# Attention, expert halves and MLP in one kernel: a weight load goes ahead in its queue, and five pieces of side work stand elsewhere in the order

## Chip, cores and metric

One core of one Trainium2 chip runs the whole program. The metric is device time in microseconds (us), the median of several runs; lower is better.

## What is computed

The reference, cut to what matters:

```
scores = matmul(q, k.T) / sqrt(64)                 # B 2, H 8, S 576, D 64
cum    = cumsum(log(clip(f, 1e-4, 1)), -1)
scores = where(causal, -1e9, scores + cum[:, None] - cum[None, :])
attn   = exp(scores - rowmax);  attn /= attn.sum + 1e-9
x      = (attn @ v) as (1152 tokens, 512)

p      = domain_probs / (domain_probs.sum + 1e-9)   # 1152 x 4
x      = sum over e of p[:, e] * (relu(x @ w1[e]) @ w2[e])      # 4 experts, F 1024

h      = x @ w_in                                   # 512 x 2048
out    = (h * sigmoid(1.702 * h)) @ w_out           # 2048 x 512
```

## The kernel before, in words

Products of fp32 numbers are made of three products in the fast rounded type fp32r: each operand is split into a rounded high part and the remainder (`xh`/`xl`, `whi`/`wlo`, `hh`/`hl`), and `high*high + high*low + low*high` is summed in PSUM. A split costs a rounding copy, mostly on ScalarE (ACT, `round_act`, L74), and a subtraction, mostly on VectorE (DVE, such as `wlo` at L263) or GpSimd (POOL). TensorE (PE) does all products; all other engines prepare its operands and take its results away.

The program has three stretches that overlap at their borders. **Attention** (to about 200 us) goes in passes of heads, in units of up to four query tiles. A unit runs through the stages scores (L674, PE), `max` (L704, DVE: adds the decay row `cb` or `cbs` and takes the row's maximum `mx`), `exp` (L720, ACT, with the row sum `sm`), `norm` (L727 and L728 on DVE, then the scaling of `e` on POOL, L730), transposes `t` (L748, PE) with their copies `ph` to SBUF (L74, ACT), the product with the values `x` (`emit_pv`, L793), and its split into `xh` and `xl` (L74 and L809). Stages of later units are issued among those of earlier ones. **Expert halves**: the four experts' hidden width of 1024 is cut in two, so that there are eight halves. They are gone through in visits (L153): 0 to 6 take a half with those token groups that the attention has finished, 7 to 9 (`v_exp` on) with two groups, 10 to 13 (`v_all` on) with all tokens. For each visit the weights `wa` (first product, L994 or L1032) and `wb` (second product, L1162) are loaded in four pieces `wst` of 512 KB in pairs (`load_pair`), and rounded to `whi` and `wlo` by `split_w` (L239). The visits 0 to 6 run among the attention's work. From visit 7 on ("joint") the first product is made by a scheme with fewer products from sums of weights (`sum_weights`, L276: four additions `sr` on POOL) and sums of tokens (`tr`, `th`, `tl`, L323 to L344), and its results are combined on DVE (`u` L1075 and L1078, `jc` L1038). Partial outputs are scaled by the token's share and added up in `acc` (L1204, L1206). **The MLP** follows; its weights are converted beforehand in small steps (`mlp_convert`, L420: `cvt`, `wf`, `cvd`) that are spread over the expert halves by a running account `cv_due`.

What sets the order: the program is written once, and each engine carries out its instructions in an order that a scheduler fixes when the program is built, from the written order and from explicit ties. `keep_order` ties one instruction behind another, `tc.issue_after` ties what is issued inside it behind an instruction, and `pin_turn` holds engines to the written order. On each engine, and in SP's queue of DMA issues, what comes later in that order can't pass what comes first, even if that still waits for a semaphore or for a free buffer.

Places that the steps below speak of: `prep_keys` (L582) splits the keys of a pair of heads (part 0 the rounding `ks`, parts 1 and 2 the subtractions for the two heads, on DVE and POOL, L593). `load_cum` (L613) loads the decay rows: two `cb` of 128 x 512 and one `cbs` in two halves, the latter into a single buffer that the pass before must have left. `attention` (L896) walks over the units and calls all of that at fixed distances (`first[k] == i + 2` is two units before a pair's first). `place` (L1348) puts side work at steps `g` of the joint products; the account of conversions is kept in the loop that emits the products (L1511).

```
for k in [k for k in nxt if first[k] == i + 2]:
    load_cum(*k)
```

Of the kernel before, what the change touches and what calls it, by code (L numbers as in the profile page):

```python
# [53 lines left out]
def attn_moe_mlp(ctx: ExitStack, tc: tile.TileContext, qk0, qk1, qk2, v0, vp, fg, dp, wa_moe, wb_moe, wa_mlp, wb_mlp, out):  # L54
# [6 lines left out]
    nc = tc.nc  # L61
# [177 lines left out]
    def split_w(kind, v_, g):  # L239
# [13 lines left out]
        if v_ == 1:  # L253
            acts = [j for j in nc.cur_bb.bb.instructions if j.engine == nc.scalar.engine]
            keep_order([first_act[0] if kind == "a" else acts[-2], acts[-1]])
        (wa if kind == "a" else wb)[v_, g] = (hi, lo)
# [338 lines left out]
    def prep_parts(p, h0):  # L595

        for part in range(3):
            prep_keys(p, h0, part)
# [14 lines left out]
    def load_cum(p, h0):  # L613

        cs, b, s0 = p
        st = pairs[p, h0]
        r = b * H + h0
        st["cb"] = [cb_p.tile([128, 512], F32, tag="cb", name="cb") for _ in range(2)]
        for g, cb in enumerate(st["cb"]):
            load(cb, cumd[r + g:r + g + 1, :512].to_broadcast([128, 512]))  # L620
        st["cbs"] = cbs_p.tile([128, S], F32, tag="cbs", name="cbs")
        for g in range(2):
            load(st["cbs"][64 * g:64 * g + 64], cumd[r + g:r + g + 1, :].to_broadcast([64, S]))
# [109 lines left out]
    def emit_tr(c, u):  # L733
# [7 lines left out]
        for k, (q0, off, w, _) in enumerate(todo):  # L741
# [3 lines left out]
            for k0, k1 in [(0, min(nk, 4))] + [(4, 5)] * (nk > 4):  # L745
# [4 lines left out]
                for j, h in enumerate(hs if w == S else hs[k:k + 1] if len(hs) > 1 else hs):  # L750
                    r = 64 if w == S else 128
                    ph = ph_of[c, h]
                    ph = ph[:, 3:4, 0:64] if k0 else ph[:, 0:k1, o:o + r]
                    if plain(c) and k1 == 2 and h < 4:
                        nc.vector.tensor_copy(ph, cols[:, :, j * r:(j + 1) * r])
                    else:
                        round_act(ph, cols[:, :, j * r:(j + 1) * r])

# [137 lines left out]
    def attention():  # L896
# [16 lines left out]
        for i in range(len(seq) + L_X2 + 1):  # L913
# [5 lines left out]
            with tc.issue_after(last_pool) if i == 0 else ExitStack():  # L919
                for k in new:  # L920
                    prep_parts(*k)
# [13 lines left out]
            for k in [k for k in nxt if first[k] == i + 2]:  # L935
                load_cum(*k)
            for k in [k for k in nxt if first[k] == i and i]:
                load_values(*k)
            for k in names:
                j = i - STAGES[k]  # L940
                if k in per_unit:
                    if 0 <= j < len(seq):
                        per_unit[k](*seq[j])
                    continue
# [403 lines left out]
    def place():  # L1348
# [6 lines left out]
        for v_ in range(v_exp, v_all):  # L1355
            b, (c1, c2) = visits[v_]
            h0, h1, l2 = (3, v_, b, c1), (3, v_, b, c2), (4, v_, b, c1)
            put(h0, 1, sum_weights, v_ + 1, 0)
# [59 lines left out]
    for i, (kind, v_, b, c) in enumerate(seq):  # L1418
# [24 lines left out]
        for g in range(n_steps):  # L1443
# [58 lines left out]
            if late:  # L1502

                if sums_at.get(u, 0) < 2:
# [6 lines left out]
                    if kind == 3 and v_ in both_joint and c == EXP[0]:  # L1511
                        cv_due[0] += g in (0, 2)
# [69 lines left out]
```

## Time and profile before

| what | value |
|---|---|
| median of 3 runs | 687.19 us (686.39 to 687.92) |
| the profiled execution | 687.35 us |
| its span, first to last instruction | 685.6 us |
| PE busy | 675.8 us (99%) |
| DVE busy | 526.8 us (77%) |
| ACT busy | 350.7 us (51%) |
| POOL busy | 239.4 us (35%) |
| mean granted TensorE clock | 1.00 |
| moved | 87.6 MB, mean 128 GB/s |

The times lie 1.75 us above the span because a run holds some work around the first and the last instruction. Busy shares are means over stretches of different kinds. A row of a timeline gives the start, the duration, the engine, the line of the program, the operation with its output and inputs, how many were taken together, and in brackets how long the engine had been idle before it and what ended the idling. Names of tiles leave out their numbers.

### The profile page before, as it was taken

How to read it: one execution, taken by the hardware profiler on the slowest of the kernel's cores; microseconds unless marked ns; L12 is line 12 of the kernel's file. 1: busy time of each engine (PE TensorE's matmuls, PEld its weight loads, DVE VectorE, ACT ScalarE, POOL GpSimd, SP SyncE). 2: the span in 40 equal slices, each digit the busy share in tenths (PEclk: the TensorE clock that was granted, in tenths of full speed). 3: DMA queues.
4: the chain of work that ended last, by engine and by line, in shares of the span. 5: the costliest groups of instructions: out<-in, count | busy, mean ns of one | idle time of the engine just before them, and what ended most of it. 6: DMA issues, size and time to landing. Idle time of an engine off the chain costs nothing.

```text
span 685.6 us, 10990 instructions
## 1 busy us (share of the span) xinstructions
PE 675.8 (99%) x3886; PEld 594.8 (87%) x3886; DVE 526.8 (77%) x1088; ACT 350.7 (51%) x816; POOL 239.4 (35%) x302
## 2 busy tenths in 40 slices
PE   8999999999999999999999999999999999999997
PEld 5698789888888898898898898898999998998986
DVE  6787877788697768776988879767699889997532
ACT  5677777776642645644336253362547453562420
POOL 6766588562333464533135323132003400120000
PEclk9999999999999999999999999999999999999999
DMA  8965754334341135153531423413332445441012
GB/s 255 325 251 199 255 187 160 106 101 139 123 119 66 58 97 169 44 180 100 169 108 49 152 77 110 125 50 98 110 109 77 168 124 162 132 155 60 1 46 93
DMA packets 41127, 87.59 MB, mean 128 GB/s; under 512 B 3784, under 2 KB 5840, under 8 KB 40816
## 3 DMA queue, kind: packets, MB, share of 16 engines
q1 hardware_dynamic: 40744, 84.75, 38.1%
q0 software_dynamic: 288, 2.10, 0.8%
q8 instruction: 31, 0.51, 0.3%
q14 instruction: 24, 0.20, 0.1%
q10 hardware_dynamic: 40, 0.04, 0.0%
HBM read 73.98 MB, written 12.88 MB: 127 GB/s over the span
## 4 chain that ended last, share of the span: by engine, by line
PE 87%; DVE 6%; ACT 2%; DMA 2%; issue 1%; POOL 0%; ACTq 0%; DVEq 0%; POOLq 0%
PE m L1162 38%; PE m L1032 22%; PE m L994 14%; PE s L674 3%; PE x L793 3%; PE t L748 3%; DVE wlo L263 1%; PE m L1012 1%; PE m L1157 1%; DMA wst<-in_wa_moe_dram 1%; DVE tr L344 1%; DMA wst<-in_wb_moe_dram 1%; ACT whi L74 1%; DVE hl L1146 1%; PE m L1317 1%
## 5 line engine op out<-in xcount | busy, mean ns | idle before, releaser
L1162 PE MATMUL m<-whi,hh 128*128 128x512 f32 x384 | 107.1, 392 | 0.0
L1162 PE MATMUL m<-wlo,hh 128*128 128x512 f32 x384 | 106.6, 391 | 0.0
L1162 PE MATMUL m<-whi,hl 128*128 128x512 f32 x384 | 105.7, 390 | 0.0
L1043 POOL TENSOR_TENSOR hl<-jc,hh 128x320 fp32r<-128x320 f32 (+1 forms) x60 | 52.6, 880 | 141.4 <-ACT hh L74 141.2
L263 DVE TENSOR_TENSOR wlo<-wst,whi 128x512 fp32r<-128x512 f32 x128 | 98.1, 781 | 4.3 <-ACT whi L74 4.0
L1162 PEld LDWEIGHTS m<-wlo,hh 128*128 128x128 f32 x384 | 71.9, 188 | 15.2
L1162 PEld LDWEIGHTS m<-whi,hl 128*128 128x128 f32 x384 | 71.9, 188 | 15.0
L74 ACT ACTIVATE whi<-wst 128x512 fp32r<-128x512 f32 x128 | 75.5, 623 | 15.2 <-PE m L1162 11.6
L1162 PEld LDWEIGHTS m<-whi,hh 128*128 128x128 f32 x384 | 70.6, 188 | 12.4
L284 POOL TENSOR_TENSOR sr<-wst 128x256 f32<-128x256 f32 x20 | 18.4, 920 | 153.0 <-DMA wst<-wm 79.5
L730 POOL TENSOR_SCALAR e<-e,sm 128x128 f32<-128x128 f32 (+4 forms) x72 | 46.3, 655 | 45.3 <-DVE sm L728 29.5
L1041 ACT ACTIVATE jc<-jc 128x320 f32<-128x320 f32 (+1 forms) x60 | 27.0, 451 | 52.5 <-DVE jc L1038 52.0
L994 PE MATMUL m<-xh,whi 128*128 128x256 f32 (+2 forms) x256 | 52.4, 317 | 0.0
L720 ACT ACTIVATE e<-e,mx 128x128 f32<-128x128 f32 (+4 forms) x72 | 41.7, 581 | 20.6 <-DVE mx L704 18.5
L994 PE MATMUL m<-xl,whi 128*128 128x256 f32 (+2 forms) x256 | 50.9, 313 | 0.0
L994 PE MATMUL m<-xh,wlo 128*128 128x256 f32 (+2 forms) x256 | 50.7, 313 | 0.0
L1206 DVE SCALAR_TENSOR_TENSOR acc<-m,dpn,acc 128x512 f32<-128x512 f32 x63 | 46.3, 742 | 4.9 <-PE m L1162 4.8
L994 PEld LDWEIGHTS m<-xh,whi 128*128 128x128 f32 x256 | 41.6, 189 | 2.2 <-issue 0.5
L994 PEld LDWEIGHTS m<-xl,whi 128*128 128x128 f32 x256 | 41.5, 189 | 0.9
L1140 ACT ACTIVATE m<-m 128x384 f32<-128x384 f32 x48 | 23.0, 480 | 36.8 <-DVE m L1038 35.1
L994 PEld LDWEIGHTS m<-xh,wlo 128*128 128x128 f32 x256 | 41.1, 189 | 0.6
L1070 ACT ACTIVATE u<-m 128x320 f32<-128x320 f32 (+2 forms) x26 | 11.2, 433 | 51.1 <-PE m L1032 51.1
(178 smaller groups left out, 1503.9 us busy)
## 6 DMA issues: line engine op xcount, KB each, us to landing
wst<-in_wa_moe_dram SPq DMA_DIRECT2D x26, 512.0 KB, 4.4
wst<-in_wb_moe_dram SPq DMA_DIRECT2D x26, 512.0 KB, 4.3
mst<-in_wa_mlp_dram SPq DMA_DIRECT2D x16, 512.0 KB, 4.2
wm<-wf SPq DMA_DIRECT2D x32, 256.0 KB, 4.0
mst<-in_wb_mlp_dram SPq DMA_DIRECT2D x16, 512.0 KB, 4.1
wst<-wm SPq DMA_DIRECT2D x16, 512.0 KB, 3.9
cb<-cumd SPq DMA_DIRECT2D x16, 256.0 KB, 4.8
qr<-in_qk_dram SPq DMA_DIRECT2D x8, 384.0 KB, 5.2
```

The source lines that it names most:

```text
L74: return nc.scalar.activation(out=out, in_=in_, func=AF.Copy)
L263: nc.vector.tensor_sub(lf, raw, f(hf))
L674: nc.tensor.matmul(pt[:, :z - a], lhsT=lr[i][0], rhs=lr[i][1], start=i == 0 and not (both and pt is not bank), stop=i == n - 1, skip_group ...
L720: nc.scalar.activation(out=e[:, off:off + w], in_=e[:, off:off + w], func=AF.Exp, scale=-1.0, bias=mx, accum_out=sm[:, 0, k:k + 1])
L730: nc.gpsimd.tensor_scalar(out=e[:, off:off + w], in0=e[:, off:off + w], scalar1=sm[:, 0, i:i + 1], scalar2=1.0, op0=ALU.mult, op1=ALU.mult)
L994: nc.tensor.matmul(p[:, :n], lhsT=w[:, k, :], rhs=x[c][:, k, :], start=(j == 0 and k == 0), stop=(j == 2 and k == 3))
L1032: nc.tensor.matmul(p[:, :WN], lhsT=w[a][:, k, :], rhs=x[z][:, k, :], start=start and j == 0 and k == 0, stop=stop and j == 2 and k == 1, s ...
L1041: nc.scalar.activation(out=r, in_=r, func=AF.Relu)
L1043: nc.gpsimd.tensor_sub(hl[:, g, :], r, f(hh[:, g, :]))
L1140: nc.scalar.activation(out=p[:, :n], in_=p[:, :n], func=AF.Gelu_apprx_sigmoid)
L1162: nc.tensor.matmul(p, lhsT=h_tile(v_, b, c, j, x, k), rhs=wb[v_, k][w].rearrange("p a c -> p (a c)"), start=i == 0 and k == 0, stop=i == 2 ...
L1206: nc.vector.scalar_tensor_tensor(out=a, in0=p, scalar=d, in1=a, op0=ALU.mult, op1=ALU.add)
```

## The change

No instruction is added or taken away; five pieces of work stand elsewhere.

1. The decay rows of the fifth pair of heads are loaded in two parts: the two `cb` as before, the two halves of `cbs` one unit later, and ahead of the latter the pending remainders of weight splits (`split_rest`) and the weight load that is due after them. The same flush of what is due happens once more, one unit after this pair's first.
2. The key subtraction on DVE (part 1) of the sixth pair is issued only behind the last DVE instruction of that step's `norm`.
3. The four roundings of the second weights (`wb`) of visit 6 are tied behind the last `ph` copy of the attention's passes of pairs (`last_copy`).
4. In the first joint visit (7) the first weight sum for the next one is put at step 5 instead of 1.
5. In visit 11 (`v_all + 1`) two conversion steps come at step 6 of the first joint product (`c == EXP[0]`) instead of one at step 0 and one at step 2.

```diff
@@ -253,6 +253,8 @@
         if v_ == 1:
             acts = [j for j in nc.cur_bb.bb.instructions if j.engine == nc.scalar.engine]
             keep_order([first_act[0] if kind == "a" else acts[-2], acts[-1]])
+        if v_ == v_exp - 1 and kind == "b":
+            keep_order([last_copy[0], [j for j in nc.cur_bb.bb.instructions if j.engine == nc.scalar.engine][-1]])
         (wa if kind == "a" else wb)[v_, g] = (hi, lo)
         if kind == "a" and v_ in joint:
             joint_raw[g] = raw
@@ -592,9 +594,9 @@
             g = part - 1
             (nc.gpsimd if g else nc.vector).tensor_sub(st["ks"][z[1 - g], g], raw[z[g]], f(st["ks"][z[g], g]))
 
-    def prep_parts(p, h0):
-
-        for part in range(3):
+    def prep_parts(p, h0, parts=range(3)):
+
+        for part in parts:
             prep_keys(p, h0, part)
 
     def prep_queries(p, h0, c, parts=(0, 1)):
@@ -612,12 +614,21 @@
 
     def load_cum(p, h0):
 
-        cs, b, s0 = p
+        load_cum_rows(p, h0)
+        load_cum_both(p, h0)
+
+    def load_cum_rows(p, h0):
+
         st = pairs[p, h0]
-        r = b * H + h0
+        r = p[1] * H + h0
         st["cb"] = [cb_p.tile([128, 512], F32, tag="cb", name="cb") for _ in range(2)]
         for g, cb in enumerate(st["cb"]):
             load(cb, cumd[r + g:r + g + 1, :512].to_broadcast([128, 512]))
+
+    def load_cum_both(p, h0):
+
+        st = pairs[p, h0]
+        r = p[1] * H + h0
         st["cbs"] = cbs_p.tile([128, S], F32, tag="cbs", name="cbs")
         for g in range(2):
             load(st["cbs"][64 * g:64 * g + 64], cumd[r + g:r + g + 1, :].to_broadcast([64, S]))
@@ -755,6 +766,10 @@
                         nc.vector.tensor_copy(ph, cols[:, :, j * r:(j + 1) * r])
                     else:
                         round_act(ph, cols[:, :, j * r:(j + 1) * r])
+        if not plain(c):
+            last_copy[:] = [j for j in nc.cur_bb.bb.instructions if j.engine == nc.scalar.engine][-1:]
+
+    last_copy = []
 
     ph_of, xf = {}, {}
 
@@ -917,8 +932,9 @@
             last_pool = [j for j in nc.cur_bb.bb.instructions if j.engine == nc.gpsimd.engine][-1]
             begin = len(nc.cur_bb.bb.instructions)
             with tc.issue_after(last_pool) if i == 0 else ExitStack():
+                late_key = [k for k in new if k == nxt[5]]
                 for k in new:
-                    prep_parts(*k)
+                    prep_parts(*k, (0, 2) if late_key else range(3))
                 for j in nc.cur_bb.bb.instructions[begin:]:
                     if i == 0 and j.engine == nc.scalar.engine:
                         keep_order([first_act[0], j])
@@ -933,7 +949,16 @@
                 for _ in range(2):
                     load_pair()
             for k in [k for k in nxt if first[k] == i + 2]:
-                load_cum(*k)
+                (load_cum_rows if k == nxt[4] else load_cum)(*k)
+            for k in [k for k in nxt if first[k] == i + 1 and k == nxt[4]]:
+                split_rest()
+                while pair_due:
+                    pair_due.pop()()
+                load_cum_both(*k)
+            if first[nxt[4]] == i - 1:
+                split_rest()
+                while pair_due:
+                    pair_due.pop()()
             for k in [k for k in nxt if first[k] == i and i]:
                 load_values(*k)
             for k in names:
@@ -941,6 +966,10 @@
                 if k in per_unit:
                     if 0 <= j < len(seq):
                         per_unit[k](*seq[j])
+                    if k == "norm" and late_key:
+                        vec = [j for j in nc.cur_bb.bb.instructions if j.engine == nc.vector.engine][-1]
+                        with tc.issue_after(vec):
+                            prep_parts(*late_key[0], (1,))
                     continue
                 fn, at = by_last[k], last
                 for key in list(at):
@@ -1355,7 +1384,7 @@
         for v_ in range(v_exp, v_all):
             b, (c1, c2) = visits[v_]
             h0, h1, l2 = (3, v_, b, c1), (3, v_, b, c2), (4, v_, b, c1)
-            put(h0, 1, sum_weights, v_ + 1, 0)
+            put(h0, 5 if v_ == v_exp else 1, sum_weights, v_ + 1, 0)
             put(h1, 1, sum_weights, v_ + 1, 1)
             for u, m in ((l2, 0), ((5, v_, b, c1), 1)):
                 put(u, -0.5, high_sums, v_ + 1, m)
@@ -1509,7 +1538,7 @@
                     else:
                         rate = (0.75 if kind == 4 else 0) if v_ < v_all else 1.4 if v_ == v_all else 1.75
                     if kind == 3 and v_ in both_joint and c == EXP[0]:
-                        cv_due[0] += g in (0, 2)
+                        cv_due[0] += 2 * (g == 6) if v_ == v_all + 1 else g in (0, 2)
                     cv_due[0] += rate * (4 / n_steps) if rate != 11 / 4 else 3 * (g < 3)
                 while cv_due[0] >= 1:
                     in_turn(next, cv_gen[0], None)
```

The order on the engines, at the places where the argument stands. First SP's queue of DMA issues at some 61 to 78 us, the piece of difference; `cb` and `cbs` are the decay rows, `wst` a pair of weight pieces, `vd`, `kq` and `qr` the values, keys and queries of the next pair of heads.

```order
 L80 DMA cb<-cumd 128x512 x2
+L80 DMA wst<-in_wb_moe_dram 128x2x512
 L80 DMA cbs<-cumd 64x576 x2
+L80 DMA vd<-in_vp_dram 128x640
 L80 DMA wst<-in_wb_moe_dram 128x2x512
-L80 DMA vd<-in_vp_dram 128x640
 L80 DMA kq<-in_qk_dram 128x576
 L80 DMA qr<-in_qk_dram 128x512
 L80 DMA qr<-in_qk_dram 128x768
-L80 DMA wst<-in_wb_moe_dram 128x2x512 x3
+L80 DMA wst<-in_wb_moe_dram 128x2x512 x2
```

One load of `wb` now stands ahead of `cbs`, the next stands where the first stood, behind the values, and two instead of three follow the queries.

Second, ACT at 67 to 82 us, before and then with the change; `whi` are roundings of weights, `ph` copies of transposes, `e` exponentials, `hh` roundings of hidden values.

```order
L74 ACTIVATE whi<-wst 128x512 x4
L74 ACTIVATE ks<-kq 64x576 x2
L720 ACTIVATE e,sm<-e,mx 128x576
L74 ACTIVATE xh<-x 128x320
L74 ACTIVATE ph<-t 128x3x128 x2
L720 ACTIVATE e,sm<-e,mx 128x384
L1145 ACTIVATE hh<-m 128x256
L720 ACTIVATE e,sm<-e,mx 128x384
L74 ACTIVATE whi<-wst 128x512 x2
L74 ACTIVATE ph<-t 128x4x128 x2
L74 ACTIVATE ph<-t 128x4x64 x2
```

```order
L74 ACTIVATE whi<-wst 128x512 x4
L74 ACTIVATE ks<-kq 64x576 x2
L74 ACTIVATE whi<-wst 128x512 x2
L731 ACTIVATE e,sm<-e,mx 128x576
L74 ACTIVATE xh<-x 128x320
L74 ACTIVATE ph<-t 128x3x128 x2
L731 ACTIVATE e,sm<-e,mx 128x384
L1174 ACTIVATE hh<-m 128x256
L731 ACTIVATE e,sm<-e,mx 128x384
L1174 ACTIVATE hh<-m 128x256
L74 ACTIVATE whi<-wst 128x512 x2
L74 ACTIVATE ph<-t 128x4x128 x2
```

Two `whi` moved ahead of the long exponential (128x576), and the next two stand, as two stood before, right ahead of the two `ph` of 4x128, now with a second `hh` in front.

Third, PE at the end of the attention, 186 to 194 us, before and then with the change: `t` are the last transposes, `x` the last products with the values, `m` the second products of visit 6 (L1162, with the change L1191) and the first of the next (L994, with the change L1023).

```order
L748 MATMUL t<-identr,e 128x128 x3
L1162 MATMUL m<-whi,hh 128x512 x4
L1162 MATMUL m<-wlo,hh 128x512 x4
L1162 MATMUL m<-whi,hl 128x512 x4
L1162 MATMUL m<-whi,hh 128x512 x4
L1162 MATMUL m<-wlo,hh 128x512 x4
L1162 MATMUL m<-whi,hl 128x512 x2
L793 MATMUL x<-ph,vd 64x320 x6
L793 MATMUL x<-ph,vd 64x192 x2
L793 MATMUL x<-ph,vd 64x64 x2
L1162 MATMUL m<-whi,hl 128x512 x2
```

```order
L759 MATMUL t<-identr,e 128x128 x3
L1191 MATMUL m<-whi,hh 128x512
L808 MATMUL x<-ph,vd 64x320 x6
L808 MATMUL x<-ph,vd 64x192 x2
L808 MATMUL x<-ph,vd 64x64 x2
L1191 MATMUL m<-whi,hh 128x512
L1023 MATMUL m<-xh,whi 128x384 x3
L1191 MATMUL m<-whi,hh 128x512 x5
L1191 MATMUL m<-wlo,hh 128x512 x2
```

The last `x` stood behind 22 of the products `m`; now they stand behind one, and the `m` with `whi` and `wlo` come after them.

## Rows read from the trace of the kernel before

**Rows 1.** busy time, share of the span and instructions by engine

```profile
PE 675.8 (99%) x3886; PEld 594.8 (87%) x3886; DVE 526.8 (77%) x1088; ACT 350.7 (51%) x816; POOL 239.4 (35%) x302
```

**Rows 2.** PE's waits over the whole run: waited for, us, times, longest

```profile
PE x L793 <- ACT ph L74: 1.0, 1, 1.0
PE t L748 <- ACT ph L74: 0.9, 1, 0.9
PE m L1032 <- DVE jc L1038: 0.7, 1, 0.7
PE m L1032 <- ACT th L74: 0.5, 1, 0.5
```

**Rows 3.** table by stretches: busy us of each engine, clock, DMA share

```profile
90.00:170.00 80.00, 80.00 (x562) 69.86 (x561) 61.53 (x196) 55.84 (x159) 48.12 (x67) 1.00 0.43 139
```

**Rows 4.** SP's timeline: start, us, operation, [idle before <- releaser]

```profile
63.72 2.54 SPq L80 DMA_DIRECT2D cb<-cumd  x2
72.12 1.10 SPq L80 DMA_DIRECT2D cbs<-cumd  x2
73.31 0.54 SPq L80 DMA_DIRECT2D wst<-in_wb_moe_dram  x1
```

**Rows 5.** ACT's timeline, 66 to 84 us

```profile
79.15 1.15 ACT L74 ACTIVATE whi<-wst 128x512 fp32r<-128x512 f32 x2 [1.43 <-DMA wst<-in_wb_moe_dram]
80.21 1.61 ACT L74 ACTIVATE ph<-t 128x512 f32<-128x512 f32 x4
```

**Rows 6.** DVE's timeline, 70 to 84 us

```profile
72.02 1.49 DVE L263 TENSOR_TENSOR wlo<-wst,whi 128x512 fp32r<-128x512 f32 x1
73.53 1.46 DVE L593 TENSOR_TENSOR ks<-kq,ks 64x576 fp32r<-64x576 f32 x1
...
75.56 0.54 DVE L704 CUSTOM_DVE_ANT_0 e<-s,cb 128x384 f32<-128x384 f32 x1
...
79.82 1.29 DVE L263 TENSOR_TENSOR wlo<-wst,whi 128x512 fp32r<-128x512 f32 x2 [1.71 <-ACT whi L74]
```

**Rows 7.** PE's timeline, 72 to 84 us

```profile
75.72 0.63 PE L748 MATMUL t<-identr,e 128*128 128x128 f32 x4 [0.39 <-DVE sm L728]
...
78.95 0.64 PE L994 MATMUL m<-xh,wlo 128*128 128x256 f32 x4
79.42 0.52 PE L994 MATMUL m<-xl,whi 128*128 128x256 f32 x3
```

**Rows 8.** DVE's timeline, 86 to 97 us

```profile
87.70 1.24 DVE L593 TENSOR_TENSOR ks<-kq,ks 64x576 fp32r<-64x576 f32 x1
...
94.94 0.75 DVE L1206 SCALAR_TENSOR_TENSOR acc<-m,dpn,acc 128x512 f32<-128x512 f32 x1 [1.35 <-PE m L1162]
```

**Rows 9.** ACT's timeline, 172 to 183 and 183 to 196 us

```profile
177.91 0.63 ACT L74 ACTIVATE ph<-t 128x256 f32<-128x256 f32 x2
...
186.67 0.49 ACT L74 ACTIVATE ph<-t 128x384 f32<-128x384 f32 x1
```

**Rows 10.** PE's timeline, 186 to 196 us

```profile
186.39 1.17 PE L1162 MATMUL m<-whi,hh 128*128 128x512 f32 x4
187.40 1.08 PE L1162 MATMUL m<-wlo,hh 128*128 128x512 f32 x4
...
191.58 2.27 PE L793 MATMUL x<-ph,vd 128*64 128x320 f32 x20
```

**Rows 11.** POOL's timeline, 205 to 226 us

```profile
219.32 0.88 POOL L1043 TENSOR_TENSOR hl<-jc,hh 128x320 fp32r<-128x320 f32 x1 [5.31 <-ACT hh L74]
```

**Rows 12.** DVE's timeline, 187 to 204 and 205 to 215 us

```profile
194.56 0.75 DVE L1206 SCALAR_TENSOR_TENSOR acc<-m,dpn,acc 128x512 f32<-128x512 f32 x1 [1.05 <-PE m L1162]
...
209.33 0.82 DVE L344 TENSOR_TENSOR tr<-xh 128x640 f32<-128x640 f32 x1
...
210.73 2.68 DVE L344 TENSOR_TENSOR tr<-tr,xl 128x640 f32<-128x640 f32 x2
```

**Rows 13.** DVE's timeline, 333 to 340 us

```profile
336.20 0.41 DVE L433 TENSOR_SCALAR cvt<-cvt 128x512 f32<-128x512 f32 x1
```

## Prediction

> **What bounds the kernel now.** I read the page's busy shares first. TensorE (PE) is busy for 99% of the span [rows 1], so almost nothing can be won except by taking away moments in which PE stands still. The view of PE's waits names them. Five lie beside the change's parts: `t` behind ACT `ph` (0.9 us), `x` behind ACT `ph` (1.0), `m` L1032 behind DVE `jc` (0.7) and behind ACT `th` (0.5) [rows 2], and `t` behind DVE `sm` (0.4, the first of [rows 7]). Together they are 3.5 us: the most that taking away waits can give. The table by stretches says where nothing can be won: from 90 to 170 us PE is busy for all of the 80 us [rows 3]. The granted clock is 1.00 there (the 2.4 GHz level) and plays no part. No engine gets more or fewer instructions; everything is a move.
>
> The sum is made against the profiled execution, 687.35 us (span 685.6 and 1.75 around it), which lies 0.16 above the median, 687.19.
>
> **Part 1: a weight load goes ahead (66 to 82 us).** Before, SP issues the two `cb` from 63.72, then stands in front of `cbs` until 72.12, and issues the `wb` load only at 73.31 [rows 4]. ACT's `whi` gets it at 79.15, after 1.43 us of idling; the `ph` copies behind it begin at 80.21 [rows 5], and PE's `t` waits 0.9 for them. After, this load stands ahead of `cbs`, so it is issued as soon as the second `cb` is out, at 63.72 + 2.54 = 66.3; with the same 5.8 us from issue to use it is there near 72. ACT rounds it before its next `e`, and DVE's two `wlo` come ahead of its next `max`. The 0.4 before `t` goes. But two things are late next.
>
> First, the `max` of DVE at 75.56 frees the buffer that the next scores take. With two `wlo` between the key subtraction (ends 73.53 + 1.46 = 74.99) and this `max`, it starts at 74.99 + 1.29 = 76.28 by the price of the pair at 79.82, or at 74.99 + 2 x 1.49 = 77.97 by that of the one at 72.02 [rows 6]; it takes 0.54, so it ends at 76.8 to 78.5. PE, counted in the new order with the durations of before, is there at about 76.3: its `t` at 75.72 would start 0.39 sooner, but six more products of 0.12 (four take 0.47 from 78.95 on) stand ahead of it, and its own four take some 0.3 [rows 7]. The new wait is 0.5 to 2.2; I take the low end, since the pair is the same work on tiles of the same kind.
>
> Second, the next `wb` load stands where the old one stood, one issue (0.54) later, with its `whi` again ahead of the `ph` copies: they start at 80.21 + 0.54 = 80.75, and `t` after one of them at about 81.3. PE comes to that `t` from 79.42 + 0.52 = 79.94 [rows 7], minus the 0.4 saved, plus 0.5 lost and 0.8 of other products placed ahead of it: 80.8. A wait of 0.5 is left. Old waits 1.3, new ones 1.0: **-0.3**; between -1.3 (no new wait at all) and +1.0 (both `wlo` dear; then PE arrives too late to wait a second time).
>
> What the rows show for a `wlo` is 1.49 us at 72.02 and 1.29 for two at 79.82 [rows 6]. The Trainium skill ("SBUF — State Buffer", section "Who interferes with whom") says that a Vector instruction with two SBUF inputs contends with a GpSimd instruction that reads SBUF, and that the one issued second is blocked until the other ends. By that rule, which speaks against this part, both `wlo` are held by GpSimd's key and query work if it still runs then, and this part costs +1.0 instead of -0.3; the spread of the two rows agrees in direction.
>
> **Part 2: the key subtraction later.** One DVE `ks` of 1.24 us at 87.70 moves behind the last `sm` of its step. There DVE idles for 1.35 us before the `acc` at 94.94 [rows 8], which covers it, and PE has no wait nearby. **0**; if the cover were half gone, +0.6.
>
> **Part 3: four weight roundings later (175 us).** ACT does four `whi` among the exponentials (a pair takes 1.15 [rows 5]) ahead of two `ph` copies, which come only at 177.91 [rows 9], and PE's `x` waits 1.0 for them. With the four `whi` (2.3 us) gone from there, `ph` can follow its `t` and that wait has no reason left: -1.0. They come back at the attention's end, one ahead of the last `ph` copies and three behind. There the order of PE is new too: the last `x` stand after one `whi,hh` product instead of after two whole groups, so PE reaches them near 186.6 (186.39 and one product of 0.25) instead of 191.58 [rows 10]. The last `ph` copy ends at 186.67 + 0.49 = 187.16 [rows 9], with one more `whi` (0.57) ahead of it near 187.7. So a new wait of 0.6 to 1.1 takes the old one's place, less what ACT gains by coming there sooner. **-0.2**, between -1.0 (ACT is early enough) and +0.1.
>
> **Part 4: the weight sum later (209 us).** GpSimd makes four `sr` in a row that ends at 219.32 - 5.31 = 214.01 [rows 11]. In that time DVE's two `tr` take 2.68 us, where one just before takes 0.82 [rows 12]: 2.68 - 2 x 0.82 = 1.04 us are lost on the way to `th`, for which PE waits 0.5. With the sum behind a later `hl` this wait goes if DVE starts its row of `tr` as before. It may not: it starts behind an `acc` at 194.56, which already waits 1.05 for PE's product, and that product now stands behind the last `x`. Counted by the new order it ends up to 1.45 us later. So the part gives between -0.5 and 1.45 - 1.04 = +0.4; **-0.4**, since up to 1.0 us of delay is still covered.
>
> **Part 5: two conversion steps later (336 us).** Two `cvt` of DVE, 0.41 each and the first at 336.20 [rows 13], stand ahead of the two `jc`, the second of which ends the wait of 0.7. Without them `jc` can come up to 0.8 sooner, more than the wait, held only by the products that it reads. They come back behind the `jc`, where DVE next waits for ACT. Between -0.7 and 0: **-0.5**.
>
> From 90 to 170 the order moves too, without a wait to win; a new one would cost up to the longest of the old, 1.0. I take 0, since DVE and ACT are busy there for only 62 and 56 of the 80 us [rows 3].
>
> Sum: -0.3 + 0 - 0.2 - 0.4 - 0.5 = -1.4. 687.35 - 1.4 = 685.95, which is **685.8** beside the median. About 0.2% (1.4 us) is what a measurement of this kernel can tell from no change, so the forecast lies right on the line between faster and same, 685.8.
>
> **Rivals.**
> - *All five waits go and none comes in their place:* 687.19 - 3.5 = 683.7. For it: each part lies beside one wait of rows 2, and PE has no other large ones. Against it: parts 1 and 3 put the same work ahead of other consumers.
> - *Each wait is only exchanged for another:* 686.4 to 687.9, about 687.2. For it: the second `wb` load takes the first's place before the same `ph`, and the attention's order is new as a whole. Against it: part 5 is free of that.
> - *Slower: the late roundings hold up the attention's end.* The four `whi` (2.3 us of ACT) and their `wlo` (0.65 each on DVE) come in one bunch with the last `hh` and `ph`. It decides if the last of them ends after PE has come to `m<-wlo,hh`, at 187.40 before [rows 10]. With all 2.3 us in the open and only part 5 won: 687.19 + 2.3 - 0.5 = 689.0. For it: PE gets to the last `x` some 5 us sooner than before. Against it: three of the four stand behind the last `ph`, and PE has the `x` to do before it needs them.
> - *The held `wlo` of part 1*, +1.3 on the forecast: 687.1.
>
> That the change would not do what it says is excluded by the order, in which each of the five pieces stands elsewhere.
>
> **How the numbers follow.** Forecast 0.42 (684.8 to 686.8), all waits gone 0.17, exchanged 0.20, slower 0.15, held `wlo` 0.06. The range leaves out about half of the best case and the far half of the slower one: 683.7 to 688.0. Faster by over 0.2%: a little over half of the forecast (0.23), the best case (0.17), 0.03 of the others: 0.43. Slower, above 688.6: the slower case without its mild end (0.13), and 0.04 of the exchanged and the held: 0.17. The rest, 0.40, is within 0.2%.
>
> **What would show it.** In the changed profile's view of PE's waits, `m` L1032 (under its new line number) behind `jc` and `th` should be gone or under 0.3 each, `t` behind `sm` gone, and a new row of `s` behind DVE's `max` of about 0.6 should show near 76 us. `x` behind `ph` should be there still, but at about 187 us instead of 178. The forecast is wrong if PE is busy for less than before in the stretch from 170 to 200, if a new wait of over 1 us shows between 90 and 170, or if DVE's two `tr` before 214 us still take over 2.2 us.

## The result and the profile after

The change takes 690.81 us (median of 4 runs, 690.33 to 691.13), the kernel before 686.79 beside it: a ratio of 1.0059 with the interval [1.0045, 1.0073]. It is **slower** by 4.0 us (3.1 to 5.0). The forecast was 685.8 and its range ended at 688.0; the time lies beyond it.

The profiled execution of the change took 690.33 us, with a span of 688.5 where [rows 1] had 685.6. The page's busy line after:

```profile
PE 676.9 (98%) x3885; PEld 595.1 (86%) x3886; DVE 528.3 (77%) x1088; ACT 350.0 (51%) x816; POOL 235.6 (34%) x302
```

PE is busy for 1.1 us more; the other 1.8 of the 2.9 us is time in which it stands. The view of PE's waits over the run (waited for, us, times, longest) names the places:

```profile
PE m L1061 <- ACT th L74: 1.8, 1, 1.8
PE s L685 <- DVE mx L715: 1.8, 1, 1.8
...
PE m L1061 <- DVE jc L1067: 0.5, 2, 0.3
...
PE x L808 <- ACT ph L74: 0.2, 1, 0.2
```

Of [rows 2], the wait of `t` behind `ph` (0.9) is gone and that of `x` behind `ph` fell from 1.0 to 0.2. The wait for `th` grew from 0.5 to 1.8, one of 1.8 behind `max` is new, and so are 0.6 behind `xh` and 0.4 behind `acc` (181.19 and 97.50 below). To see where the 2.9 us arise, one sets the same products side by side, one execution of each kernel. PE's timeline before (start, duration, operation, in brackets idle time and releaser):

```profile
97.62 2.16 PE L793 MATMUL x<-ph,vd 128*64 128x320 f32 x16
...
186.15 0.49 PE L748 MATMUL t<-identr,e 128*128 128x128 f32 x3
...
210.90 0.45 PE L1032 MATMUL m<-xh,whi 128*128 128x320 f32 x2
...
214.24 0.56 PE L1032 MATMUL m<-th,sh 128*128 128x320 f32 x2 [0.54 <-ACT th L74]
...
215.50 0.46 PE L1032 MATMUL m<-xh,whi 128*128 128x320 f32 x2
...
217.26 1.09 PE L1162 MATMUL m<-whi,hh 128*128 128x512 f32 x4
...
339.08 0.46 PE L1032 MATMUL m<-xl,sh 128*128 128x320 f32 x2
...
355.31 0.46 PE L1032 MATMUL m<-xh,whi 128*128 128x320 f32 x2
```

The same view of the change:

```profile
78.09 0.50 PE L685 MATMUL s<-ks,qhi 128*128 128x512 f32 x1 [1.76 <-DVE mx L715]
...
97.50 0.62 PE L1023 MATMUL m<-xh,whi 128*128 128x256 f32 x3 [0.43 <-DVE acc L1235]
98.05 2.16 PE L808 MATMUL x<-ph,vd 128*64 128x320 f32 x16
...
181.19 0.39 PE L1023 MATMUL m<-xh,whi 128*128 128x256 f32 x1 [0.59 <-ACT xh L74]
...
187.15 0.49 PE L759 MATMUL t<-identr,e 128*128 128x128 f32 x3
...
212.36 0.45 PE L1061 MATMUL m<-xh,whi 128*128 128x320 f32 x2
...
216.93 0.56 PE L1061 MATMUL m<-th,sh 128*128 128x320 f32 x2 [1.76 <-ACT th L74]
...
218.19 0.46 PE L1061 MATMUL m<-xh,whi 128*128 128x320 f32 x2
...
341.32 0.46 PE L1061 MATMUL m<-xl,sh 128*128 128x320 f32 x2
...
357.23 0.51 PE L1061 MATMUL m<-xh,sh 128*128 128x256 f32 x2 [0.23 <-DVE jc L1067]
...
358.04 0.46 PE L1061 MATMUL m<-xh,whi 128*128 128x320 f32 x2
```

| the same products | before | change | behind by |
|---|---|---|---|
| the 16 `x` after part 1 | 97.62 | 98.05 | 0.43 |
| the last `t` of attention | 186.15 | 187.15 | 1.00 |
| the first joint products | 210.90 | 212.36 | 1.46 |
| after the wait for `th` | 215.50 | 218.19 | 2.69 |
| after `jc` of part 5 | 339.08 | 341.32 | 2.24 |
| after the next `jc` | 355.31 | 358.04 | 2.73 |
| span | 685.6 | 688.5 | 2.9 |

At 98 us the change is only 0.43 behind, although it has waited 1.76 for `max`: the execution before had waited there too, 0.9 behind `ph` and 0.4 behind `sm`. Most profiles with this load in its old place don't have the 0.9 (see the experiments), so part 1 costs more than this table shows. The largest step is the one across the wait for `th`, 1.23 us. Part 5 wins 0.45 and loses 0.49 again at the next `jc`, 16 us later. DVE's timeline of the change shows what was late at the two large waits:

```profile
75.17 2.40 DVE L265 TENSOR_TENSOR wlo<-wst,whi 128x512 fp32r<-128x512 f32 x2
77.48 0.54 DVE L715 CUSTOM_DVE_ANT_0 e<-s,cb 128x384 f32<-128x384 f32 x1
...
95.40 1.27 DVE L595 TENSOR_TENSOR ks<-kq,ks 64x576 fp32r<-64x576 f32 x1
96.70 0.75 DVE L1235 SCALAR_TENSOR_TENSOR acc<-m,dpn,acc 128x512 f32<-128x512 f32 x1
...
188.73 3.50 DVE L265 TENSOR_TENSOR wlo<-wst,whi 128x512 fp32r<-128x512 f32 x3
...
192.16 0.41 DVE L371 TENSOR_TENSOR rs<-rsa,rs 128x256 fp32r<-128x256 f32 x1
...
195.41 0.75 DVE L1235 SCALAR_TENSOR_TENSOR acc<-m,dpn,acc 128x512 f32<-128x512 f32 x1 [1.31 <-PE m L1191]
...
196.41 0.82 DVE L346 TENSOR_TENSOR tr<-xh 128x640 f32<-128x640 f32 x1
...
214.42 1.69 DVE L346 TENSOR_TENSOR tr<-tr,xl 128x640 f32<-128x640 f32 x2
```

The two `wlo` ahead of `max` took 2.40 us. The moved `ks` stands ahead of the `acc` for which PE waits 0.43. And DVE's row of `tr` begins behind an `acc` that waits 1.31 for PE's product, and behind two `rs` (remainders of other sums of tokens, L369, with the change L371), the first of which (192.16) stands behind the three `wlo`; the second comes at 196.07. Of the two `acc` of this stretch, before at 190.62 and 194.56 [rows 12], this is the first; the other comes at 197.14. Before, two `tr` stood ahead of the second `acc` and began early, and the first `rs` had not been held up:

```profile
187.53 0.96 DVE L369 TENSOR_TENSOR rs<-rsa,rs 128x256 fp32r<-128x256 f32 x1 [0.35 <-ACT rs L74]
...
191.83 0.82 DVE L344 TENSOR_TENSOR tr<-xh 128x640 f32<-128x640 f32 x1
192.69 0.82 DVE L344 TENSOR_TENSOR tr<-tr,xl 128x640 f32<-128x640 f32 x1
```

### The profile page after: what moved, and what is told of

Same layout as the page of the kernel before. It is cut to its first block, busy times and chain, and to the rows that moved or that the text cites. A ratio compares the mean times of both kernels' runs of the same rounds, so it can differ in the third digit from the quotient of the medians.

```text
span 688.5 us, 10983 instructions
## 1 busy us (share of the span) xinstructions
PE 676.9 (98%) x3885; PEld 595.1 (86%) x3886; DVE 528.3 (77%) x1088; ACT 350.0 (51%) x816; POOL 235.6 (34%) x302
## 4 chain that ended last, share of the span: by engine, by line
PE 83%; DVE 10%; ACT 3%; DMA 2%; issue 1%; POOL 0%; DVEq 0%; POOLq 0%; ACTq 0%
PE m L1191 36%; PE m L1061 22%; PE m L1023 14%; PE s L685 3%; PE x L808 3%; PE t L759 2%; DVE wlo L265 2%; DVE tr L346 1%; DVE acc L1235 1%; PE m L1041 1%; DMA wst<-in_wa_moe_dram 1%; PE m L1186 1%; DVE hl L1175 1%; DVE cvd L447 1%; ACT e L731 1%
## 5 line engine op out<-in xcount | busy, mean ns | idle before, releaser
L1191 PE MATMUL m<-whi,hh 128*128 128x512 f32 x384 | 107.6, 393 | 0.0
L1191 PE MATMUL m<-wlo,hh 128*128 128x512 f32 x384 | 106.7, 391 | 0.0
L1191 PE MATMUL m<-whi,hl 128*128 128x512 f32 x384 | 105.5, 390 | 0.0
L265 DVE TENSOR_TENSOR wlo<-wst,whi 128x512 fp32r<-128x512 f32 x128 | 102.4, 814 | 2.8 <-ACT whi L74 2.4
L1191 PEld LDWEIGHTS m<-whi,hl 128*128 128x128 f32 x384 | 72.1, 188 | 15.1
L1191 PEld LDWEIGHTS m<-wlo,hh 128*128 128x128 f32 x384 | 71.8, 188 | 15.0
L1191 PEld LDWEIGHTS m<-whi,hh 128*128 128x128 f32 x384 | 70.7, 188 | 12.6
L741 POOL TENSOR_SCALAR e<-e,sm 128x128 f32<-128x128 f32 (+4 forms) x72 | 43.7, 620 | 44.9 <-DVE sm L739 31.5
L1023 PE MATMUL m<-xh,whi 128*128 128x256 f32 (+2 forms) x256 | 52.9, 318 | 1.0 <-ACT xh L74 0.6
L1023 PE MATMUL m<-xl,whi 128*128 128x256 f32 (+2 forms) x256 | 50.5, 314 | 0.0
L1023 PE MATMUL m<-xh,wlo 128*128 128x256 f32 (+2 forms) x256 | 50.3, 313 | 0.0
L1023 PEld LDWEIGHTS m<-xh,whi 128*128 128x128 f32 x256 | 41.7, 189 | 3.8 <-ACT xh L74 0.8
L1023 PEld LDWEIGHTS m<-xl,whi 128*128 128x128 f32 x256 | 41.2, 189 | 0.7
L1023 PEld LDWEIGHTS m<-xh,wlo 128*128 128x128 f32 x256 | 41.1, 189 | 0.7
```

The costliest lines, as they stand in the source:

```text
L265: nc.vector.tensor_sub(lf, raw, f(hf))
L741: nc.gpsimd.tensor_scalar(out=e[:, off:off + w], in0=e[:, off:off + w], scalar1=sm[:, 0, i:i + 1], scalar2=1.0, op0=ALU.mult, op1=ALU.mult)
L1023: nc.tensor.matmul(p[:, :n], lhsT=w[:, k, :], rhs=x[c][:, k, :], start=(j == 0 and k == 0), stop=(j == 2 and k == 3))
L1191: nc.tensor.matmul(p, lhsT=h_tile(v_, b, c, j, x, k), rhs=wb[v_, k][w].rearrange("p a c -> p (a c)"), start=i == 0 and k == 0, stop=i == 2 ...
```

## Experiments

Each ratio is to the kernel before, run beside it, whose median was 686.4 to 686.7. us are the ratio less one, times that median.

### The five parts, each alone

Each kernel keeps one of these pieces of the diff and undoes the others: `only_load`, `key_alone`, `only_round`, `only_sum`, `only_conv`.

```diff
-                load_cum(*k)
+                (load_cum_rows if k == nxt[4] else load_cum)(*k)
...
-                    prep_parts(*k)
+                    prep_parts(*k, (0, 2) if late_key else range(3))
...
+        if v_ == v_exp - 1 and kind == "b":
+            keep_order([last_copy[0], [j for j in nc.cur_bb.bb.instructions if j.engine == nc.scalar.engine][-1]])
...
-            put(h0, 1, sum_weights, v_ + 1, 0)
+            put(h0, 5 if v_ == v_exp else 1, sum_weights, v_ + 1, 0)
...
-                        cv_due[0] += g in (0, 2)
+                        cv_due[0] += 2 * (g == 6) if v_ == v_all + 1 else g in (0, 2)
```

> Part 1 alone (the wb load ahead of cbs, both flushes), all else as before. Theory A (two sources: part 1 makes PE wait for a max behind two wlo; part 3 puts four wlo where DVE is the bound): +0.5 to +1.5 us against before, with a wait of the scores behind DVE mx of 1.5 to 2.0 near 78 us in place of the two waits of t. Theory B (the loss comes only when the parts meet): within 0.5 us of before, and no wait over 1 us. Theory C (part 4 is the loser): within 0.5 us.

> Part 2 alone (the key subtraction of DVE behind the norm). All theories: within 0.5 us of before; this closes the sum of the five parts, which by the four measured ones is +1.6 + 2.9 - 1.1 + 0.2 = about +3.6 of the +4.0 of the whole change.

> Part 3 alone (four weight roundings of visit 6 behind the last ph copy). Theory A: +1.5 to +3 us; the wait of x behind ph at 178 is gone, but the wait of m behind th near 215 grows from 0.5 to over 2.5 (the weight sum still slows two tr there), since four wlo fall between 186 and 193 us, ahead of DVE's run of tr. Theory B: within 0.5 us. Theory C: -1 to 0 us, because the wait for ph goes and nothing else is late.

> Part 4 alone (the weight sum at step 5 instead of 1). Theory A and B: -0.3 to -0.9 us; the two tr before 214 us take 1.7 instead of 2.7 and the wait behind th is gone. Theory C: +1 us or more, because the sum then comes late for the next visit's sums, with a new wait after 225 us.

> Part 5 alone (two conversion steps at step 6). Theory A: the wait behind jc at 338 falls from 0.7 to about 0.2, and a new one of about 0.25 comes near 352 us as in the changed kernel: -0.5 to 0 us. Theories B and C: -0.5 to 0 us as well; this run sizes the term.

| part alone | ratio | interval | us | PE's wait for `th` or, after it, `tl` |
|---|---|---|---|---|
| 1, load | 1.0023 | [1.0013, 1.0033] | +1.6 | 0.5 |
| 2, key | 0.9995 | [0.9981, 1.0009] | -0.3 | 0.5, for `tl` |
| 3, roundings | 1.0042 | [1.0028, 1.0055] | +2.9 | 2.6 |
| 4, sum | 0.9984 | [0.9971, 0.9998] | -1.1 | none |
| 5, conversions | 1.0003 | [0.9994, 1.0011] | +0.2 | 0.5, for `tl` |

The sum of the parts is +3.3, the change itself +4.0 (3.1 to 5.0): within the intervals it is the sum. Parts 1 and 3 make the loss. Part 4 is the only gain, and a narrow one: its interval ends just below 1, and its median, 686.22, is 0.3 under that of before. With part 1 alone PE waits behind `max` twice, 1.5 at 78 us and 0.9 at 98 us. With part 4 alone, DVE's timeline has the pair of `tr` at 210.23 with 1.68 instead of the 2.68 of [rows 12].

One more thing shows here: the wait of 0.9 at which part 1 aimed is in none of these five profiles, even where part 1 is undone. With part 2 alone SP's timeline has the `wb` load issued behind `cbs` as before, and ACT's `whi` begins 4.3 us later without a wait for it, where [rows 4] and [rows 5] have 5.8 us from the issue to `whi`:

```profile
72.68 0.54 SPq L80 DMA_DIRECT2D wst<-in_wb_moe_dram  x1
```

```profile
76.99 1.14 ACT L74 ACTIVATE whi<-wst 128x512 fp32r<-128x512 f32 x2
```

Ten profiles have this load in the old place. In three PE waits there: before, `x_first` and `round_pool`, 0.9, 1.1 and 0.5 us, where the load landed 5.8, 5.9 and 5.3 us after its issue. In the other seven it landed after 3.9 to 4.4 us, and PE doesn't wait.

### Part 1 with its two `wlo` behind `max`

```diff
+        max_of[c, u] = [j for j in nc.cur_bb.bb.instructions if j.engine == nc.vector.engine][-1]
...
+            if kind == "b" and v_ == 2 and g < 2:
+                keep_order([max_of[1, ((6, 7), (256,))], [j for j in nc.cur_bb.bb.instructions if j.engine == nc.vector.engine][-1]])
```

> Part 1 alone, with its two wlo tied behind the max of the next unit (both heads), so that the load is as early as in the change but DVE makes the max first. Theory A (the max behind two dear wlo is what part 1 costs): the 1.45 us wait of s behind mx near 78 us is gone, and the time falls from the 1.6 us above before of part 1 alone to within 0.6 us of before; what is left is the second wait near 98 us. Theory D (the early load itself costs, by the transfers that it delays or by the whi ahead of an exponential): the time stays 1 us or more above before.

Measured: 0.9989 [0.9975, 1.0004], no difference from before and 2.3 us less than part 1 as it was. Both waits behind `max` are gone. PE waits for something else there, `e` of POOL's scaling; the first row is PE's, the second DVE's:

```profile
77.82 0.66 PE L762 MATMUL t<-identr,e 128*128 128x128 f32 x4 [1.35 <-POOL e L744]
```

```profile
75.34 1.90 DVE L263 TENSOR_TENSOR wlo<-wst,whi 128x512 fp32r<-128x512 f32 x2
```

So the loss of part 1 is the place of two instructions in DVE's order; that the pair runs ahead of `max` is what costs, 2.41 us with part 1 alone and 2.40 in the change; behind `max` its 1.90 cost nothing that shows. Having the load early wins nothing that can be measured.

### Part 3 with the roundings nearer, and on GpSimd

`round_near` ties the four `whi` behind the two `ph` for which PE waits at 178 us, not behind the attention's last. `round_pool` is part 3 with the four `wlo` on GpSimd. `sum_near` is `round_near` with part 4.

```diff
-        if not plain(c):
+        if c == 2:
             last_copy[:] = [j for j in nc.cur_bb.bb.instructions if j.engine == nc.scalar.engine][-1:]
...
-            nc.vector.tensor_sub(lf, raw, f(hf))
+            (nc.gpsimd if (kind, v_) == ("b", v_exp - 1) else nc.vector).tensor_sub(lf, raw, f(hf))
```

> Part 3 alone, but the four roundings tied behind the two ph copies that PE waits for at 178 us instead of behind the last one of the attention; PE's order is as before but for four rows. Theory A (part 3 loses by putting four wlo into DVE's full stretch from 186 us on): the wait of x behind ph goes, the wlo fall at about 179 to 182 where DVE then idles, the wait behind th stays at 0.5: -0.6 to -1.1 us. Theory E (the roundings cost wherever they come after that copy, because ACT is late with what follows): 0 to +1 us.

> Part 4 (weight sum at step 5) with part 3 in the nearer form of round_near. Theory A: the two gains add, -1.1 - 0.9 = about -2 us against before (684.5), neither the wait behind ph nor that behind th shows. If one hides the other: no better than part 4 alone (-0.3 us by its medians, -1.1 by the ratio).

> Part 3 alone as in the change, but the four wlo of these weights are made by GpSimd instead of DVE; the same numbers. Theory A: the wait behind th falls from 2.6 back to under 1.3, and the time from 2.4 us above before to under 1 us above. Theory F (the loss is the new order of PE at the attention's end, where DVE's acc waits for a product that now stands behind the last x): the wait behind th stays over 2 us and the time about 2 us above before.

Measured: `round_near` 0.9998 [0.9986, 1.0009], `sum_near` 0.9994 [0.9976, 1.0012], `round_pool` 1.0079 [1.0056, 1.0101]. The gains expected of `round_near` (0.6 to 1.1) and of `sum_near` (about 2) didn't come. Its wait for `ph` is gone and that for `th` is the old 0.5, but ACT now does the four `whi` (first row) ahead of the `e` and `xh` for which PE then waits (second row):

```profile
176.27 2.19 ACT L74 ACTIVATE whi<-wst 128x512 fp32r<-128x512 f32 x4
```

```profile
179.97 0.39 PE L1014 MATMUL m<-xh,whi 128*128 128x256 f32 x1 [1.52 <-ACT xh L74]
```

The 1.0 of `x` behind `ph` is exchanged for 1.5 behind `xh`; in the change itself 0.6 comes at the same place. `sum_near` has the same 1.5 and, without a wait for `th`, is no better than part 4 alone. `round_pool` was meant to take the `wlo` from DVE and so shorten the wait for `th`. It became 3.8. This speaks against the `wlo` as its cause, but settles nothing: GpSimd's sums came late as well (the first `sr` at 190.17 instead of 186.78).

### Is it DVE's load, or PE's order?

Two causes were left for the longer wait for `th`: three `wlo` of 3.50 us that hold up DVE before its row of `tr`, or PE's order, in which the last `x` come ahead of the `m` products, so that DVE's `acc` gets its product later. `dve_dummy` is the kernel before with four extra subtractions on DVE, tied ahead of the first `rs`. `x_first` is the kernel before with one tie on the last `x`, and leaves the roundings early. The tie was to put the last `x` behind one product of visit 6, as the change has them. In its trace they stand behind 13 (before 22, in the change 1), so it is a weaker form of that order.

```diff
+                for _ in range(4):
+                    nc.vector.tensor_sub(spare, f(h11[:, :, :240]), f(h12[:, :, :240]))
...
+                keep_order(made + [[j for j in nc.cur_bb.bb.instructions if j.engine == nc.vector.engine][-1]])
```

```diff
+        if v_ == v_exp - 1 and last_x:
+            keep_order([last_x.pop(), [j for j in nc.cur_bb.bb.instructions if j.engine == nc.tensor.engine][-11]])
```

> The kernel before with four more subtractions of two SBUF tiles (128x480, about the size of a wlo, into a spare tile that nobody reads) on DVE between 185.6 and 187.5 us, where part 3 brings its four wlo; all other engines keep their order. Theory A (DVE's amount of work up to th decides, so the four wlo of part 3 are its price): the wait of m behind th grows from 0.5 to 2 or more and the time by 1.5 to 2.3 us. Theory F (DVE there waits for PE's product before its acc anyway; part 3 loses because that product comes later): DVE's idle of about 1.1 before rs and 1.05 before the acc takes most of the four, th waits 0.5 to 1.3, the time is 0 to 0.8 us above before.

> The kernel before with one tie more: the last products x of the attention stand, as with the change, behind one product of visit 6's second products instead of behind 22; its weights are rounded as early as before, so neither ACT nor DVE gets work later. Theory F (part 3 loses because PE's product comes later, DVE waits for it before its acc, and its tr are queued behind): the wait behind th grows from 0.5 to 1.5 to 2.6 and the time by 1.0 to 2.5 us. Theory A (DVE's four late wlo): th waits 0.5 as before, the time is within 0.5 us of before.

Measured: `dve_dummy` 1.0019 [1.0007, 1.003], `x_first` 1.0053 [1.0039, 1.0066]. The first lost 1.3 us, between what the two causes were expected to give; the second 3.6, more than either. With the extra work DVE is held for nearly as long as in the change (three in 3.16 us, first row), and PE's wait for `th` stays short (second row, PE's):

```profile
185.43 3.16 DVE L375 TENSOR_TENSOR spare<-xh 128x480 f32<-128x480 f32 x3
```

```profile
213.52 0.55 PE L1061 MATMUL m<-th,sh 128*128 128x320 f32 x2 [0.38 <-ACT th L74]
```

That does not clear the work, though: PE comes to `th` late itself, since it has waited 0.8 behind an `xl` of DVE (L833), and the last pair of `tr` took 2.10 there instead of 2.68. `x_first` has the long wait with nothing but that tie added. Its `x` on PE, then DVE's timeline, then PE's at `th`:

```profile
189.54 2.27 PE L808 MATMUL x<-ph,vd 128*64 128x320 f32 x20
```

```profile
194.57 0.75 DVE L1230 SCALAR_TENSOR_TENSOR acc<-m,dpn,acc 128x512 f32<-128x512 f32 x1 [1.75 <-PE m L1184]
...
195.57 0.82 DVE L344 TENSOR_TENSOR tr<-xh 128x640 f32<-128x640 f32 x1
196.43 0.82 DVE L344 TENSOR_TENSOR tr<-tr,xl 128x640 f32<-128x640 f32 x1
```

```profile
216.43 0.64 PE L1054 MATMUL m<-th,sh 128*128 128x320 f32 x2 [2.71 <-ACT th L74]
...
221.00 1.09 PE L1184 MATMUL m<-whi,hh 128*128 128x512 f32 x4
```

The two `tr` that began at 191.83 and 192.69 now begin at 195.57 and 196.43, behind an `acc` that waits for PE, and the wait for `th` grows by 2.17. The `acc` itself is no later than before (194.57 and 194.56): with the tie the scheduler put DVE's rows the other way round, and that is what costs.

The executions don't run level, so the table counts from the start of PE's last three `t`, the same instruction in each (us; the last two rows are DVE's time up to that `th`):

| | before | `dve_dummy` | `x_first` | part 3 alone | change |
|---|---|---|---|---|---|
| the last `t` starts at | 186.15 | 184.47 | 186.14 | 184.54 | 187.15 |
| DVE's first `rs` | 1.38 | 4.04 | 1.44 | 5.01 | 5.01 |
| DVE's first `tr` | 5.68 | 8.36 | 9.43 | 9.25 | 9.26 |
| ACT's `th` that PE waits for | 27.30 | 28.26 | 29.50 | 29.81 | 28.99 |
| DVE busy | 24.9 | 26.5 | 24.8 | 27.6 | 26.7 |
| DVE standing | 2.4 | 1.8 | 4.7 | 2.3 | 2.2 |

In `x_first` DVE does no more than before and stands 2.3 us longer: the order alone is enough to make `th` 2.2 us late. In part 3 alone it is the other way: DVE stands no longer than before and is busy 2.7 us longer (the change has part 4's saving in it). There the late `wlo` reach the `tr` on a path of their own. They hold up the first `rs`; ACT can round the next one only when the first has been copied out, and DVE's second `rs`, with the `tr` behind it, needs that rounding. ACT's row of this rounding in the change; before, it came at 191.04, behind the same transfer:

```profile
195.11 0.42 ACT L74 ACTIVATE rs<-rsb 128x256 fp32r<-128x256 f32 x1 [4.13 <-DMA tsd<-rs]
```

In the change this rounding ends at 195.53, and PE's product lets the `acc` begin at 195.41: the two paths to the `tr` come out within 0.2 us of each other. So this much is shown: part 3 loses because DVE's `tr` begin 3.6 us late, and either of its two effects alone makes them late, PE's and DVE's new order (`x_first`, 3.7 us) or late work ahead of the first `rs` (`dve_dummy`, 2.7 us). They don't cost the same: in `x_first` `th` comes 2.2 later, in `dve_dummy` only 1.0, in part because its last pair of `tr` is 0.6 cheaper. How much of part 3's loss would stay if only one of the two were taken away, no run shows; that the paths end so close together suggests that most of it would.

### The parts that are worth having

`sum_tied` is part 4 with `load_tied`; `mended` has parts 2 and 5 besides. Part 3 is in neither.

> Part 4 with part 1 in the form of load_tied (the two wlo behind the max). If the gains of the two places add: -1.1 - 0.75 = about -1.9 us against before (ratio 0.9973), below both kernels. If load_tied's gain was chance: about -1.1 (ratio 0.9984).

> The whole change without part 3 and with part 1's two wlo behind the max (parts 1 tied, 2, 4, 5). If parts 1 and 3 hold the whole loss: -1.5 to -2.5 us against before, that is 5.5 to 6.5 us below the change. If the parts disturb one another: above before.

Measured: 685.25 us, 0.9978 [0.9969, 0.9988], and 685.54 us, 0.9982 [0.9973, 0.9992]. Both are faster than the kernel before, by 1.5 and 1.2 us, and than the change, by over 5; between the two nothing can be told. In neither does PE wait for `th`.

## Why the prediction was wrong

**What bounds it** was right: PE is busy for 98 to 99% of the span, and all that moved is its waits. Beside them hardly anything was to be won, and what was put in front of other consumers had to cost.

**Part 1**, forecast -0.3, measured +1.6 alone. The mechanism stood in the text: two `wlo` ahead of `max`, PE waits for the scores' buffer. The mis-sized term is the price of the pair. I took the low end, 1.29, "since the pair is the same work on tiles of the same kind", and it took 2.40. The dear price forecast `max` at 77.97 and a wait of up to 2.2; `max` started at 77.48 and the wait was 1.76. The Trainium skill's rule ("SBUF — State Buffer", "Who interferes with whom") was quoted against this part, and the +1.0 worked out with it had the right sign; the trace agrees with the rule. The pair of 1.29 ran at 79.82, while GpSimd stood idle (first row below, GpSimd before); that of 2.40 ran at 75.17 beside GpSimd's key subtraction, which ended at 76.41 (second row, GpSimd in the change), and 76.41 with the undisturbed 1.29 behind it is 77.70, where the pair ended at 77.57. No run here took GpSimd's work away from beside this pair.

```profile
81.29 0.15 POOL L698 MEMSET e<- 128x64 f32 x1 [1.84 <-PE m L994]
```

```profile
74.60 1.81 POOL L595 TENSOR_TENSOR ks<-kq,ks 64x576 fp32r<-64x576 f32 x1
```

The second wait forecast, 0.5 at `t`, didn't come, since PE arrived late, as the dear case said. Two things were missed: a further wait near 97 us (alone 0.9 behind a second `max`, in the change 0.4 behind an `acc`), and that the 0.9 to be won rested on one execution, in which the load took 5.8 us. That the sum was made against this execution was bad luck, and could not be seen from one profile.

**Part 2**, forecast 0, measured -0.3 with an interval across zero: right. In the change its cover is partly gone, as the text said it might be: `ks` at 95.40 stands ahead of the `acc` for which PE waits 0.43.

**Part 3**, forecast -0.2, measured +2.9 alone. The first half was right: the wait of `x` behind `ph` went, and the new one at the attention's end is 0.2, under the 0.6 to 1.1 forecast. The sum stopped at that wait. It followed the last `x` and `ph`, but not the `m` products that the `x` now push back, nor who on DVE waits for those, nor what stands on DVE behind the late `wlo`.

**Part 4**, forecast -0.4, measured -1.1 alone. The mechanism was right, 2.68 became 1.69. But here the step that failed is written down: "up to 1.0 us of delay is still covered". I had named the `acc` and given it up to 1.45 us of delay, and DVE's wait for PE's product ends at 195.41 instead of 194.56, only 0.85 later. What failed is the assumption that this delay is all, and that DVE's row of `tr` begins behind the `acc` before as well. Two `tr` stood ahead of it; with part 3 they come behind it, and behind an `rs` that the late `wlo` hold up: the first one moved from 191.83 to 196.41, by 4.6 us. With part 4's 1.0 subtracted, PE still waits 1.8.

**Part 5**, forecast -0.5, measured +0.2 with an interval across zero. The wait of 0.7 shrank to 0.3, as forecast. The clause that failed is "They come back behind the `jc`, where DVE next waits for ACT": in the change they delay DVE until the next `jc`, where PE waits 0.23 and loses the 0.45 again (table above). With part 5 alone PE gets to the same product 0.21 later again after having won 0.47; such a net gain is within the interval, so the term was too large rather than of the wrong sign.

**The rival on the slow side** had the right part and the right stretch with 689.0, and a chance of 0.15, but only half of the mechanism: it had ACT's and DVE's late weights hold up `m<-wlo,hh`. The change's waits show none there; what the late weights hold up is `rs`, and with it `tr`. Its argument against, that "PE has the `x` to do before it needs them", was true for PE and left out the other engines.

**The signs.** The two that named a row spoke: `th` was to be gone or under 0.3 and is 1.8, `s` behind `max` was to be about 0.6 and is 1.8. The three under which the forecast was to be wrong stayed silent (PE's busy time from 170 to 200 us is 29.1 after 29.0, the longest wait between 90 and 170 is 0.4, the two `tr` take 1.69): they looked where the loss was not.

## What to carry to other kernels

When a moved piece of work lets the scheduler turn two rows of one engine round, follow the row that fell behind to its consumers, not only the one that came forward: on an engine that works in order, one instruction waiting late holds back all that stands behind it, and the price is how far those moved. To tell such a wait from added work, count the engine's busy and standing time up to the late row, from an instruction that is the same in each execution. Price work that goes ahead of a critical instruction at the dearest row of its kind, above all beside a busy GpSimd. A wait seen in one profile may depend on how long a transfer took in that execution; look at it in several before counting it as something to win.

## What the runs showed of the hardware beside this

After two of its longest waits PE ran at a lower clock for a while: 2.71 us in `x_first` and 3.82 in `round_pool`, both with stretches at 0.50. The table by stretches of `x_first` (stretch, length, busy us of PE, PE's loads, DVE, ACT and POOL, granted clock, DMA share, GB/s):

```profile
205.00:213.00 8.00, 8.00 (x42) 6.96 (x41) 7.19 (x11) 1.48 (x2) 0.59 (x1) 1.00 0.22 68
213.00:216.00 3.00, 0.72 (x5) 0.45 (x4) 2.54 (x3) 0.36 (x1) 3.00 (x3) 1.00 0.00 0
216.00:218.00 2.00, 1.43 (x5) 1.03 (x6) 1.59 (x2) 1.74 (x4) 0.92 (x2) 0.70 0.00 0
218.00:220.00 2.00, 2.00 (x8) 2.00 (x9) 2.00 (x5) 0.00 (x0) 0.00 (x0) 0.50 0.00 0
220.00:222.00 2.00, 2.00 (x12) 1.83 (x12) 1.32 (x3) 1.06 (x3) 0.04 (x1) 0.95 0.48 78
```

PE was busy for all of the 8 us before, stood for most of 213 to 216, and came back to a granted clock that fell to 0.50, the 1.2 GHz level, from 218 to 220. From 216.43 to 221.00 it needed 4.57 us for nine pairs that took 3.02 before (214.24 to 217.26): 1.55 us on top of the 2.19 by which it began later, together the 3.7 between the two spans (689.3 and 685.6). So in this execution a wait of 2.71 us cost 1.55 more, and of the 3.6 that `x_first` lost this is the part that the order does not explain. It does not follow every wait of this length. `only_round` waited 2.59 in its profile, and the clock stayed:

```profile
218.00:220.00 2.00, 2.00 (x13) 1.74 (x11) 1.95 (x5) 0.38 (x1) 0.00 (x0) 1.00 0.42 19
```

Of its five runs four have a mean clock of 0.998 or 0.999 and took 688.1 to 689.3 us; the fifth has 0.995 and took 690.8. The change's profiled execution has no such stretch either (mean clock 1.00, wait 1.76), but its three other runs have a mean of 0.997 and spans of 688.7 to 689.4; that they lost it at the same place was not seen, since only one execution has a trace. How the 4.0 us divide between the wait for `th`, the clock after it and part 1 is therefore known from the single parts alone.
